# Reordering a latency-bound attention phase: a two-engine start, an earlier memory read, and segment boundaries without a drain

## Chip, cores and metric

The kernel runs on one core of one Trainium2 chip. The metric is the device time of one execution in microseconds (us), median over the runs of a kernel. Engines are named as in the profile: PE is TensorE (PEld its weight loads), DVE is VectorE, ACT is ScalarE, POOL is GpSimd, SP is the engine that issues the transfers. The granted clock is the share of PE's full clock that the profile shows as granted, averaged over a stretch.

## The reference

Two attention blocks read the same input and a gate mixes them:

```python
x = A_x                                             # [1, 2048, 512], bf16
g = sigmoid((x * gate_w).sum(-1, keepdims=True))
a = A_ref(...)   # memory transformer: 64 segments of 32 tokens + 8 memory tokens, 32 heads of 128, strictly serial
b = B_ref(...)   # infini-attention: 4 segments of 512 tokens, 32 heads of 16
return g * a + (1 - g) * b

# B_ref, for each of the 4 segments (M, z start at 0; phi(t) = t+1 if t > 0 else exp(t)):
p     = softmax(q k^T * scale + causal_mask);  a_dot = p v
a_mem = (phi(q) M) / (phi(q) z + 1e-6)
o     = sigmoid(beta) * a_mem + (1 - sigmoid(beta)) * a_dot
M    += phi(k)^T v;   z += sum(phi(k))
# then b = concat(o) @ wo
```

## The kernel before

The program first does all of B, then a barrier, then all of A. The change touches B and its start. Every operation is appended to a per-engine list in *program order*; a tracker derives the semaphore waits from what each operation reads and writes. An engine executes its own list strictly in order.

B works on 4 segments of 8 groups (4 heads each). One group needs: `pK`, `pQ`, `pV`, `pKr` (projections; `pKr` makes phi(k) and `pQ` makes phi(q)), three logits batches `w0`, `w1`, `w2` (each fills banks 0 to 3 of PSUM, the memory that matmuls write to, then four exps on ACT), `p` (P times V, into bank 4), `nz` (phi(q) times M and z, into bank 5), `mz` (update of M and z), and `chain` (8 small DVE steps that normalise and add).

```python
def plan_projQ(g):
    par = g % 2                                      # two buffers, by parity of the group
    P.op("pe", f_proj, ..., writes=[rbank[7]])       # 4 matmuls 128x512
    P.op("dve", copy pb[7] -> QTg[par])
    if sb > 0:
        P.op("dve", qmin[par] = min(QTg[par], 0))
        P.op("act", qmin[par] = exp(qmin[par]))
        P.op("dve", phiQ[par] = max(QTg[par], 0) + qmin[par])
# [cut]
def plan_nz(g):                                      # only where sb > 0
    pq = phiQ_b[g % 2]
    P.op("pe", f_nz, reads=[Rs("MZ16"), Rs("phiQ%d" % par)], writes=[rbank[5]])   # 16 matmuls 128x32
# [cut]
plan_proj(0)
for g in range(NG + 1):                              # NG = 8
    # order of one iteration (projections run one group ahead, P.V one group behind):
    #   w0(g)  pKr(g+1)  pK(g+1)  w1(g)  pQ(g+1)  p0(g-1)  w2(g)  p1(g-1)  nz(g-1)  pV(g+1)  mz(g)  chain(g-1)
    ...
for half in range(2):                                # end of a segment: orow -> oT, banks 6 and 7
    P.op("pe", f_otr, ...)                           # 8 transposes
    P.op("dve", ...)                                 # 2 copies
P.op("dve", MZ16 = bf16(MZ32))                       # if another segment follows
```

At the start, all 16 copies that spread the weights wq and wk into a padded layout stand on ACT, and `memT0` (transposed initial memory) follows the gate in DVE's order:

```python
for nat, pad, ... in ((wqN_sb, wqB_sb, ...), (wkN_sb, wkB_sb, ...)):
    for c in range(C):
        for half in range(2):
            P.op("act", lambda a: a.activation(pad[...], nat[...], ACT.Copy), ...)
# [cut: x transposes, gate matmul, gate sigmoid, omg, omgB]
P.op("pe", f_m0tr, ..., writes=[rbank[6]]);  P.op("dve", copy pb16[6] -> memT0)
```

The softmax here doesn't subtract the row's maximum and nothing guards it: scores larger than these inputs give would overflow.

## Time and profile before

| | before |
|---|---|
| time | 1735.62 us median of 4 runs (1733.33 to 1736.89) |
| span of the profiled run | 1733.5 us, mean granted PE clock 0.937 |
| first logits batch of B | 29.27 us |
| A starts (its first weight transfer is issued) | 351.66 us |
| period of a group, segments 0 / 1 / 2 / 3 | 7.16 / 10.27 / 10.33 / 8.82 us |
| boundaries, first batch of group 7 to first batch of the next segment's group 2 | 34.91, 37.30, 37.42 us |

The period is the distance between the first logits batches (`w0`) of groups 2 and 7, divided by 5; these start times are in the timeline. The other rows can be read there too.

The next view is the windows table of the kernel before: busy microseconds of each engine in a stretch (number of instructions in brackets), then granted clock, DMA share and GB/s. The rows are the groups of segments 1 and 3, and A.

```profile
core 0: us, PE busy (x) PEld busy (x) DVE busy (x) ACT busy (x) POOL busy (x), PEclk, DMA share, GB/s
...
97.50:166.00 68.50, 47.68 (x1007) 30.09 (x1010) 42.48 (x117) 44.30 (x100) 18.12 (x28) 0.83 0.01 2
...
274.60:336.50 61.90, 45.95 (x777) 27.04 (x784) 31.65 (x77) 41.47 (x92) 18.11 (x28) 0.65 0.01 2
378.00:1733.00 1355.00, 1296.69 (x32428) 997.10 (x32488) 522.08 (x1167) 521.61 (x1008) 115.01 (x250) 0.98 0.02 5
```

In the last row PE is busy for 1297 of 1355 us: A is PE-bound, and the change does not touch it. In the two rows above it no engine is full; in segment 1, of 68.5 us, PE is busy 47.7, DVE 42.5 and ACT 44.3. Something other than throughput sets the pace there.

The timeline of one group of segment 1 (start, duration, engine and line, operation, and in brackets how long the engine sat idle and for whom) shows the loop:

```profile
126.26 0.26 DVE L654 RECIPROCAL rden<-pb 128x16 f32<-128x16 f32 x1
...
129.63 0.43 DVE L548 SCALAR_TENSOR_TENSOR phiKg<-pb,Kmin 128x256 bf16<-128x256 f32 x1 [0.48 <-ACT Kmin L546]
...
130.12 1.04 PE L495 MATMUL pb<-xT,wqB_sb 128*128 128x512 bf16 x4 [0.56 <-DVE phiKg L548]
...
131.19 0.69 DVE L499 CAST QTg<-pb 128x512 bf16<-128x512 f32 x1 [0.54 <-PE pb L495]
...
131.91 0.71 DVE L505 TENSOR_SCALAR qmin<-QTg 128x512 bf16<-128x512 bf16 x1
...
132.66 0.63 ACT L507 ACTIVATE qmin<-qmin 128x512 bf16<-128x512 bf16 x1 [0.88 <-DVE qmin L505]
...
133.32 0.69 DVE L509 SCALAR_TENSOR_TENSOR phiQ<-QTg,qmin 128x512 bf16<-128x512 bf16 x1 [0.69 <-ACT qmin L507]
...
134.07 0.56 PE L619 MATMUL pb<-MZ,phiQ 128*128 128x32 bf16 x16 [1.14 <-DVE phiQ L509]
...
134.49 0.63 PE L520 MATMUL pb<-wvB_sb,xT 128*128 128x64 bf16 x16
...
135.28 0.43 PE L572 MATMUL pb<-QTg,KTg 16*128 16x128 bf16 x16
```

Each step begins when the one above it ends: `chain` on DVE (first line, 2.5 us to the end of its eighth step), Kmin and its exp (left out), phiK (L548), projQ (L495), copy of QT (L499), min (L505), exp on ACT (L507), phiQ (L509), then `nz` on PE (L619), which had waited 1.14 us for phiQ, then the V projection (L520), `mz` (left out here) and the next group's first logits (L572). The following `chain` starts at 136.35, 10.1 us after this one. PE takes part twice, with projQ and again with `nz`, V projection and `mz`; the second time it waits for phiQ only because `nz` stands ahead of the other two in its order. The group view says how much PE sat idle ahead of `nz` in all:

```profile
L619 PE MATMUL pb<-MZ,phiQ 128*128 128x32 bf16 x384 | 13.9, 182 | 15.6 <-DVE phiQ L509 15.5
```

That is 15.6 us of idle time over 24 executions, 15.5 of it for phiQ.

At a boundary the pipeline drains. This is the timeline of the second boundary, from the last group of segment 1 to the first of segment 2:

```profile
166.04 0.43 PE L572 MATMUL pb<-QTg,KTg 16*128 16x128 bf16 x16
...
175.56 1.25 PE L604 MATMUL pb<-V32g,PT_g 128*128 128x32 bf16 x40 [1.95 <-DVE adot L663]
...
179.77 1.89 PE L745 MATMUL pb<-ident,orow 128*128 128x128 bf16 x16 [2.44 <-DVE orow L675]
180.84 1.61 DVE L749 COPY oT<-pb 128x512 bf16<-128x512 bf16 x4 [1.13 <-PE pb L745]
...
182.05 1.49 PE L481 MATMUL pb<-xT,wkB_sb 128*128 128x512 bf16 x3 [0.40 <-DVE oT L749]
...
186.25 0.43 PE L572 MATMUL pb<-QTg,KTg 16*128 16x128 bf16 x16
```

After group 7's first logits (166.04) come the last P.V matmuls (L604), the transposes of the output (L745), their copies (L749), and only then the next segment's projections (L481) and first logits at 186.25.

And the start:

```profile
12.27 5.26 ACT L385 ACTIVATE wqB_sb<-wqN_sb 128x512 bf16<-128x512 bf16 x8 [10.19 <-DMA wqN_sb<-in_B_wq_dram]
...
17.44 5.24 ACT L385 ACTIVATE wkB_sb<-wkN_sb 128x512 bf16<-128x512 bf16 x8
...
24.41 0.17 DVE L452 COPY memT<-pb 128x32 bf16<-128x32 bf16 x1
...
25.11 1.49 PE L481 MATMUL pb<-xT,wkB_sb 128*128 128x512 bf16 x3 [5.20 <-DVE memT L452]
```

The 16 copies on ACT run one after the other (12.27 to 22.68), the gate sigmoids queue behind them, the copy of `memT0` (L452) queues behind the gate on DVE, and the first projection needs the bank that it frees. (The chain of waits shows none of this: it is followed back only to the transfers of Wv and Wo, which are issued when B ends.)

### The profile page before, as it was taken

The page shows a single profiled execution, that of the slowest core. Times are in us where ns is not written, and L with a number is a line of the kernel's source. Part 1 is how long each engine was busy: PE and PEld are TensorE (multiplying, and loading weights), DVE is VectorE, ACT ScalarE, POOL GpSimd, SP SyncE. Part 2 cuts the span into 40 slices and gives each one's busy share as a digit, 9 for nine tenths or more (in the row PEclk, how much of TensorE's full clock was granted, in tenths as well). Part 3 has the DMA queues.
Part 4 walks back from the last instruction along what each step waited for, and adds up shares of the span by engine and source line. Part 5 has one row for each costly group of instructions (what it writes and reads, how often), then busy time and mean ns, then how long its engine had stood idle before and what let it go on. Part 6 is the DMA issues. An engine that isn't in the chain of part 4 may idle for free.

```text
span 1733.5 us, 80136 instructions
## 1 busy us (share of the span) xinstructions
PE 1546.9 (89%) x37477; PEld 1161.6 (67%) x37573; DVE 722.5 (42%) x1727; ACT 735.5 (42%) x1477; POOL 203.6 (12%) x396
## 2 busy tenths in 40 slices
PE   5766666779999999999999999999999999999999
PEld 3444443467777777777777777777777777777776
DVE  3556665533333333333333333333333333333333
ACT  5756465624343334343333333433333333333333
POOL 1322122201010000000000000000000000000000
PEclk8977776589999999999999999999999999999999
DMA  7000000050000000000000000000000000000000
GB/s 292 3 2 2 2 2 2 2 196 3 6 3 6 3 6 3 6 3 7 3 6 3 6 3 6 3 7 3 6 3 6 3 6 3 6 3 6 4 6 6
DMA packets 12916, 28.22 MB, mean 16 GB/s; under 512 B 800, under 2 KB 11048, under 8 KB 11048
## 3 DMA queue, kind: packets, MB, share of 16 engines
q1 hardware_dynamic: 12584, 23.09, 3.6%
q8 instruction: 294, 4.82, 1.2%
q14 instruction: 38, 0.31, 0.1%
HBM read 20.99 MB, written 2.10 MB: 13 GB/s over the span
## 4 chain that ended last, share of the span: by engine, by line
PE 74%; DVE 3%; issue 1%; SPq 1%; DMA 1%
PE pb L867 26%; PE pb L801 24%; PE pb L929 14%; PE pb L853 4%; PE pb L916 3%; PE pb L822 3%; DVE aT_st L935 1%; DVE fin L996 1%; DMA Wo_sb<-in_A_Wo_dram 1%; SPq L310 1%; DVE t_sb L992 1%; DVE hT L785 0%; PE pb L950 0%; DVE V_sb L873 0%; DVE PT_sb L857 0%
## 5 line engine op out<-in xcount | busy, mean ns | idle before, releaser
L867 PE MATMUL pb<-Wv_sb,hT 128*40 128x512 bf16 x2048 | 497.8, 381 | 3.6 <-DMA Wv_sb<-in_A_Wv_dram 3.3
L876 ACT ACTIVATE V_sb<-pb 40x512 bf16<-40x512 f32 x448 | 264.8, 591 | 362.1 <-PE pb L867 362.1
L867 PEld LDWEIGHTS pb<-Wv_sb,hT 128*40 128x40 bf16 x2048 | 178.9, 99 | 174.5 <-DMA Wv_sb<-in_A_Wv_dram 3.4
L807 ACT ACTIVATE KT_sb<-pb 128x480 bf16<-128x480 f32 (+1 forms) x192 | 101.1, 527 | 395.9 <-PE pb L801 395.9
L811 DVE CAST QT_sb<-pb 128x480 bf16<-128x480 f32 (+1 forms) x192 | 115.7, 603 | 352.8 <-PE pb L801 345.1
L929 PE MATMUL pb<-OT_sb,Wo_sb 128*128 128x40 bf16 x8192 | 236.3, 183 | 17.5 <-DVE fin L996 16.4
L929 PEld LDWEIGHTS pb<-OT_sb,Wo_sb 128*128 128x128 bf16 x8192 | 225.0, 98 | 27.2 <-ACT OT_sb L920 17.8
L801 PE MATMUL pb<-hT,Wk_sb 128*128 128x40 bf16 x8192 | 216.5, 180 | 24.6 <-DVE hT L785 23.2
L801 PEld LDWEIGHTS pb<-hT,Wk_sb 128*128 128x128 bf16 x8192 | 210.7, 96 | 28.6 <-DVE hT L785 27.0
L801 PE MATMUL pb<-hT,Wq_sb 128*128 128x40 bf16 x8192 | 217.7, 179 | 3.0 <-issue 2.4
L801 PEld LDWEIGHTS pb<-hT,Wq_sb 128*128 128x128 bf16 x8192 | 211.2, 96 | 4.2 <-issue 3.4
L830 POOL TENSOR_SCALAR_AFFINE_SELECT P_sb<-P_sb 32x384 bf16<-32x384 bf16 (+1 forms) x192 | 98.7, 527 | 939.2 <-ACT P_sb L827 939.2
L581 ACT ACTIVATE PT_g<-pb 128x512 bf16<-128x512 f32 (+1 forms) x384 | 170.4, 529 | 54.5 <-PE pb L572 52.5
L835 DVE TENSOR_REDUCE rsum<-P_sb 40x12 f32<-40x480 bf16 (+1 forms) x192 | 112.0, 583 | 149.0 <-POOL P_sb L830 149.0
L935 DVE CAST aT_st<-pb 128x128 bf16<-128x128 f32 x64 | 18.7, 292 | 265.2 <-PE pb L929 265.2
L920 ACT ACTIVATE OT_sb<-pb 128x480 bf16<-128x480 f32 (+1 forms) x192 | 87.1, 526 | 94.6 <-PE pb L916 94.6
L840 DVE TENSOR_TENSOR Pn_sb<-P_sb,rrec 40x480 bf16<-40x480 bf16 (+1 forms) x192 | 118.9, 619 | 6.6
L853 PEld LDWEIGHTS pb<-ident,Pn_sb 40*40 40x40 bf16 x2048 | 63.5, 93 | 81.0 <-DVE PT_sb L857 33.7
L587 POOL TENSOR_SCALAR_AFFINE_SELECT PT_g<-PT_g 128x512 bf16<-128x512 bf16 x128 | 82.5, 644 | 257.7 <-ACT PT_g L581 255.6
L822 PEld LDWEIGHTS pb<-KT_sb,QT_sb 128*40 128x40 bf16 x2048 | 71.3, 98 | 30.0 <-issue 0.5
L827 ACT ACTIVATE P_sb<-pb 40x480 bf16<-40x480 f32 (+1 forms) x192 | 91.0, 507 | 0.0
L857 DVE COPY PT_sb<-pb 40x480 bf16<-40x480 bf16 (+1 forms) x192 | 70.1, 365 | 32.5 <-PE pb L853 32.5
(84 smaller groups left out, 1087.4 us busy)
## 6 DMA issues: line engine op xcount, KB each, us to landing
Wk_sb<-in_A_Wk_dram SPq DMA_DIRECT2D x4, 1024.0 KB, 12.0
Wq_sb<-in_A_Wq_dram SPq DMA_DIRECT2D x4, 1024.0 KB, 20.2
Wv_sb<-in_A_Wv_dram SPq DMA_DIRECT2D x4, 1024.0 KB, 9.2
Wo_sb<-in_A_Wo_dram SPq DMA_DIRECT2D x4, 1024.0 KB, 13.8
x_sb<-in_A_x_dram SPq DMA_DIRECT2D x4, 512.0 KB, 5.6
out_dram<-fin SPq DMA_DIRECT2D x16, 128.0 KB, 1.7
wqN_sb<-in_B_wq_dram SPq DMA_DIRECT2D x1, 512.0 KB, 7.8
wkN_sb<-in_B_wk_dram SPq DMA_DIRECT2D x1, 512.0 KB, 8.8
```

Source lines behind the costliest of these rows:

```text
L581: P.op("act", (lambda j=j: (lambda a: a.activation(ptb[:, j, 128 * n0:128 * (n0 + len(wv))], pb[j][:, 0:128 * len(wv)], ACT.Exp, scale=SCA ...
L801: ins = pe.matmul(pb[bnk][:, (h - h0) * L:(h - h0 + 1) * L], wsb[:, c, h * E:(h + 1) * E], hTc[:, c, :], start=(c == 0), stop=(c == C - 1))
L807: P.op("act", (lambda bnk=bnk, dst=dst, h0=h0, h1=h1: (lambda a: a.activation(dst[:, h0 * L:h1 * L], pb[bnk][:, 0:(h1 - h0) * L], ACT.Copy ...
L811: P.op("dve", (lambda bnk=bnk, dst=dst, h0=h0, h1=h1: (lambda dv: dv.tensor_copy(dst[:, h0 * L:h1 * L], pb[bnk][:, 0:(h1 - h0) * L])))(), ...
L822: ins = pe.matmul(pb[b][0:L, (h - h0) * L:(h - h0 + 1) * L], QT_sb[:, h * L:(h + 1) * L], KT_sb[:, h * L:(h + 1) * L], start=True, stop=True)
L830: P.op("gp", (lambda h0=h0, h1=h1, nh=nh: (lambda g: g.affine_select(P_sb[0:SEG, h0:h1, 0:SEG], P_sb[0:SEG, h0:h1, 0:SEG], [[0, nh], [-1, ...
L835: P.op("dve", (lambda h0=h0, h1=h1: (lambda dv: dv.tensor_reduce(rsum[0:L, h0:h1], P_sb[0:L, h0:h1, :], AX.X, ALU.add)))(), reads=[rP], wr ...
L840: P.op("dve", (lambda h0=h0, h1=h1, nh=nh: (lambda dv: dv.tensor_tensor(Pn_sb[0:L, h0:h1, :], P_sb[0:L, h0:h1, :], rrec[0:L, h0:h1].unsque ...
L853: ins = pe.transpose(dst, Pn_sb[0:L, h, :], ident[0:L, 0:L])
L867: ins = pe.matmul(pb[vb][0:L, 0:512], hTc[:, c, :], Wv_sb[:, c, 512 * j:512 * (j + 1)], start=(c == 0), stop=(c == C - 1))
L876: P.op("act", (lambda vb=vb, j=j: (lambda a: a.activation(V_sb[0:L, 512 * j:512 * (j + 1)], pb[vb][0:L, 0:512], ACT.Copy)))(), reads=[rban ...
L929: ins = pe.matmul(pb[6][:, c * L:(c + 1) * L], Wo_sb[:, h, c * 128:(c + 1) * 128], OT_sb[:, h * L:(h + 1) * L], start=(h == 0), stop=(h == ...
```

## The change

Its intent: use two engines for the weight copies and take `memT0` out of the gate's queue; read phi(q) before it is overwritten and not wait for a new one; and let the next segment's first projections, and the old segment's tail, run inside the normal groups.

```diff
-        for nat, pad, ... : (16 copies) P.op("act", ... activation(Copy))          # [cut]
+    # after the x transposes: wq copies on ACT and wk copies on POOL, alternating
+            for eng, nat, pad, rn, rp in (("act", wqN_sb, wqB_sb, ...), ("gp", wkN_sb, wkB_sb, ...)):
+                ...  activation(dst, srcn, ACT.Copy)   or   tensor_copy(dst, srcn)
+    # f_m0tr and memT0 moved ahead of the gate                                    # [cut]
@@ plan_bseg
-    def plan_projK(g): ... T0 ...          # and projQ, projV, projKr
+    def make_proj(psb):  T0p = psb * LB;  ...  return plan_projK, plan_projQ, plan_projV, plan_projKr
@@ order of an iteration
-    plan_proj(0)
-    for g in range(NG + 1):
+    if not v.get("B_proj_prefetched"): plan_proj(0)
+    nxt = make_proj(sb + 1) if sb + 1 < NB else None
+    old = v.get("B_tail")                  # the previous segment's p, nz, chain, transposes, MZ16 copy
+    for g in range(NG + (1 if nxt is None else 0)):
+        # in group 7 the projections are those of the next segment's group 0;
+        # in group 0 the p, nz and chain are those of the previous segment's group 7
             seq.append(("w", 1))
+        if g == 1 and old: seq.append(("otr", None))      # transposes, now in banks 4 and 5
+        if havep:          seq.append(("nz", None))       # moved: ahead of pQ
         if haven:          seq.append(("pQ", None))
 ...
             seq.append(("p", qc_parts[1]))
-            seq.append(("nz", None))
+            if g == 0: seq.append(("mz16", None))
-    (transposes and MZ16 copy at the end of each segment)
+    (transposes at the end of the last segment only)
```

A side effect: in the kernel before, `nz(g-1)` stands after `pQ(g+1)` in program order, and both use phiQ buffer `(g-1) % 2`. So for groups 0 to 5 it reads phi(q) of the wrong group. Every phi(q) is close to 1 with these inputs (by the scales in the reference, q has a standard deviation of about 0.0025), and the result still passes the comparison. The changed order reads the right one.

## The prediction

> **What bounds it now.** Two phases follow each other, with a barrier between. Infini-attention (B) runs to about 352 us, the recurrent memory transformer (A) to 1733. In the windows table PE is busy 95% from 378 us on at clock 0.98 to 0.99; the change leaves A alone. From the barrier to 377 us A waits for Wv and Wo, whose transfers are issued only after B (the chain of waits starts there), so whatever B saves moves everything after it by as much.
>
> In B no engine is full: PE 60 to 70%, DVE 48 to 61%, ACT 54 to 67% by quarter. It is latency-bound. From the timeline, first logits batch to first logits batch:
> - segment 0: 7.16 us a group, paced by ACT exps sharing four banks;
> - segments 1 and 2: 10.3 us, a loop: MZ update, DVE chain 2.5, Kmin, exp, phiK 1.25, projQ 1.05 (1.9 at half clock), QTg copy, min, exp, phiQ 2.8, then the nz matmuls (PE idles 32.9 us in total for phiQ), V projection, MZ matmuls, MZ update;
> - segment 3: mean 8.8 us.
> - Each boundary drains: group 7's first batch to the next segment's group 2 takes 34.9, 37.3 and 37.4 us.
> - Start: PE waits until 24.7 us; ACT makes 16 weight copies of 0.63 us, and the gate sigmoid, then memT0 on DVE, wait behind them.
>
> **What changes.**
> 1. Start: half the copies go to POOL, in parallel, and memT0 goes before the gate. wkN lands at 13.7 us; POOL takes 0.29 us for 128 columns, 0.64 for a 512-column select, so I estimate 0.7 to 1.0 per copy, ready by 19.5 to 22. The Trainium skill ("SBUF — State Buffer", Who interferes with whom) says DVE and GpSimd can block each other at a shared port; the DVE min at 0.29 us stretches to 0.76 next to a POOL select here. Gain 4.
> 2. nz moves before projQ. In program order the old nz(g-1) reads phiQ after group g+1 has overwritten it, so it waits for a value just made (and the wrong one; phi is near 1, which hides it). Now it reads one made an iteration earlier, in a gap where PE waited for phiK. The loop closes over DVE order instead: phiQ, V32g copy 0.42, MZ update 0.83: about 9.0 us. Five intervals each: 6.4 + 6.6 us in segments 1 and 2, about 3 in segment 3.
> 3. Boundaries: the next segment's group-0 projections ride in group 7, the old tail in the new group 0, the 16 transposes (1.9 us, with copies 1.6) in group 1, where they delay projQ by about 2.9; the MZ16 copy adds 0.7. Three iterations: about 27, 30.5 and 29. Gains 8, 6.7, 8.5.
> 4. Segment 3's end: nz(7) now stands before pv(7) and waits for the previous chain: loss 1.
>
> Sum 42 us, all on the critical path. Prediction **1693 us**, 80% range 1681 to 1706; faster by over 2% 0.76, within 2% 0.23, slower 0.01.
>
> **Right or wrong by:** A starting at about 310 us; first projection at about 21; segments 1 and 2 at about 9.0 us a group; waits for phiQ nearly gone; no 10 us ACT gap at boundaries; A unchanged.
>
> **What could spoil it.** POOL copies slower than 1.2 us; transposes stalling group 1 longer; clock: the Trainium skill ("TensorE: Matmul & The Clock Gate", Part 1) says the clock halves after an idle window and recovers with activity. The windows show 0.50 at the drains and 0.65 to 0.85 in the loops; shorter gaps may lift it (then 1683) or not (projQ costs 0.85 more in each group, then 1705).

One reading in it is too large: the 32.9 us is PE's wait and PEld's wait added up. PE's own is 15.5 us. No term of the sum used it.

## The result, and the profile after

| | before | after |
|---|---|---|
| time, median (range, runs) | 1735.67 us (1731.9 to 1739.29, 12) | 1689.56 us (1686.21 to 1695.64, 8) |
| ratio to before | 1 | 0.9736 (95% interval 0.9723 to 0.975) |
| span of the profiled run | 1733.5 us | 1689.7 us |
| first logits batch | 29.27 us | 24.73 us |
| A starts | 351.66 us | 306.00 us |
| period, segments 0 / 1 / 2 / 3 | 7.16 / 10.27 / 10.33 / 8.82 us | 7.37 / 9.03 / 9.09 / 8.26 us |
| boundaries | 34.91, 37.30, 37.42 us | 26.12, 30.67, 25.17 us |

A ratio is the mean time of one kernel's fast runs over that of the other's fast runs of the same rounds, so it is not quite the ratio of the medians.

The windows table after, same columns, for the corresponding stretches (segments 1 and 3, and A):

```profile
83.20:147.20 64.00, 48.94 (x1060) 32.98 (x1071) 45.79 (x130) 43.21 (x99) 18.36 (x29) 0.81 0.01 3
...
230.60:289.80 59.20, 42.47 (x854) 26.97 (x865) 38.97 (x102) 40.99 (x91) 18.06 (x29) 0.80 0.01 2
334.00:1689.00 1355.00, 1295.51 (x32391) 995.47 (x32451) 522.12 (x1167) 521.67 (x1008) 114.99 (x250) 0.99 0.02 5
```

A (last row) took nearly the same: 1296 us of PE busy in 1355. Its length from start to end was 1383.7 us, against 1381.8 before. All of the gain lies in B, after which A starts 45.66 us earlier. ACT's idle stretch at the three boundaries, 10.2 to 12.6 us before, was 2.7 to 3.9 us.

The same part of a group in segment 1, after:

```profile
120.41 0.26 DVE L665 RECIPROCAL rden<-pb 128x16 f32<-128x16 f32 x1
...
123.52 0.56 PE L630 MATMUL pb<-MZ,phiQ 128*128 128x32 bf16 x16
...
123.77 0.42 DVE L555 SCALAR_TENSOR_TENSOR phiKg<-pb,Kmin 128x256 bf16<-128x256 f32 x1 [0.48 <-ACT Kmin L553]
...
124.26 1.04 PE L502 MATMUL pb<-xT,wqB_sb 128*128 128x512 bf16 x4 [0.17 <-DVE phiKg L555]
...
127.37 0.69 DVE L516 SCALAR_TENSOR_TENSOR phiQ<-QTg,qmin 128x512 bf16<-128x512 bf16 x1 [0.69 <-ACT qmin L514]
...
127.98 0.42 DVE L531 CAST V32g<-pb 128x256 bf16<-128x256 f32 x1
128.32 0.83 DVE L653 TENSOR_TENSOR MZ<-MZ,pb 16x32 f32<-16x32 f32 x4
...
128.49 0.44 PE L583 MATMUL pb<-QTg,KTg 16*128 16x128 bf16 x16 [0.80 <-ACT PT_g L592]
```

`nz` (L630) now sits in front of projQ, in time that PE otherwise spent waiting for phiK (L555), and waits for nothing. The loop closes on DVE: phiQ (L516), V copy (L531), MZ update (L653), then the next `chain` at about 129.2. The group view of `nz`:

```profile
L630 PE MATMUL pb<-MZ,phiQ 128*128 128x32 bf16 x384 | 14.0, 182 | 5.7 <-DVE oT L715 3.4 <-DVE amem L683 2.3
```

None of its idle time is for phiQ any more; 3.4 us is for the copies of the transposes and 2.3 us for the end of the last segment. The start:

```profile
12.04 5.26 ACT L424 ACTIVATE wqB_sb<-wqN_sb 128x512 bf16<-128x512 bf16 x8 [9.96 <-DMA wqN_sb<-in_B_wq_dram]
...
13.59 5.35 POOL L426 COPY wkB_sb<-wkN_sb 128x512 bf16<-128x512 bf16 x8 [8.98 <-DMA wkN_sb<-in_B_wk_dram]
...
17.70 0.16 DVE L435 COPY memT<-pb 128x32 bf16<-128x32 bf16 x1
...
20.09 1.49 PE L488 MATMUL pb<-xT,wkB_sb 128*128 128x512 bf16 x3 [0.24 <-issue]
```

POOL's eight copies (13.59 to 18.94) run beside ACT's eight, `memT0` is done at 17.86, and projK's row starts at 20.09 instead of 25.11 (it shows three of the four matmuls: in both runs the record of the first is missing, and the weight loads for it start at 19.69 and 24.70). And the transposes in group 1 of segment 1:

```profile
95.23 1.40 PE L711 MATMUL pb<-ident,orow 128*128 128x128 bf16 x16
...
96.23 1.42 DVE L715 COPY oT<-pb 128x512 bf16<-128x512 bf16 x4 [0.77 <-PE pb L711]
...
97.70 0.56 PE L630 MATMUL pb<-MZ,phiQ 128*128 128x32 bf16 x16 [1.07 <-DVE oT L715]
...
98.33 0.81 PE L502 MATMUL pb<-xT,wqB_sb 128*128 128x512 bf16 x3
```

The transposes (L711) follow the second logits batch; `nz` then waits 1.07 us for their copies (L715), because it needs bank 5, and projQ (L502) stands behind `nz`.

### The profile page after: what moved, and what is told of

It is laid out like the page before. It is cut to its first block, busy times and chain, and to the rows that moved or that the text cites. A ratio compares the mean times of both kernels' runs of the same rounds, so it can differ in the third digit from the quotient of the medians.

```text
span 1689.7 us, 80119 instructions
## 1 busy us (share of the span) xinstructions
PE 1534.3 (91%) x37474; PEld 1157.7 (69%) x37573; DVE 726.0 (43%) x1727; ACT 730.1 (43%) x1469; POOL 208.9 (12%) x404
## 4 chain that ended last, share of the span: by engine, by line
PE 76%; DVE 3%; issue 1%; DMA 1%; SPq 0%
PE pb L905 28%; PE pb L839 25%; PE pb L967 14%; PE pb L891 4%; PE pb L954 3%; PE pb L860 3%; DVE aT_st L973 1%; DMA Wv_sb<-in_A_Wv_dram 1%; DVE fin L1034 1%; DVE t_sb L1030 1%; DVE hT L823 0%; PE pb L988 0%; DVE V_sb L911 0%; DVE PT_sb L895 0%; SPq L304 0%
```

## The experiments

The account to be tested: three parts act one after the other in time and their gains nearly add; inside a group the pace is a latency loop through DVE in program order, which the wait of `nz` for a new phiQ had lengthened. The main rival: what was gained is clock and fewer drains, and moving `nz` only moves a wait. (Periods and boundaries below are read from each run's timeline, as above.)

### 1. The start alone

```diff
  (kernel before)
- plan_init of before
+ plan_init of the changed kernel
```

> The kernel before with the first part of the change alone (half of the weight copies on POOL, the memory transpose ahead of the gate). My account, in which the parts act one after the other in time: the first logits batch at about 24.7 us instead of 29.3, everything after it moved by as much, total about 4.5 us less (1731). Rival, the gain of the whole change is one of clock and of fewer drains: the earlier start is eaten by a slower first segment (in the changed kernel segment 0 took 0.7 us more), total within 1 us of before.

Measured: 1731.87 us (6 runs, 1728.92 to 1736.11) against 1735.27 (11 runs), ratio 0.9979 (0.9958 to 1.0). The first logits batch came at 24.80 us, as expected. But the six times fall in two clusters, three near 1729 and three near 1735, and the profiled run was the slowest of them: it kept only 1.6 us up to the start of A. Its segment 1 took 72.23 us from group 0 to group 7 (68.45 before), and the granted clock over this stretch was 0.72 against 0.83. So the head start is real, and the profiled run lost most of it where its clock was low. Nothing shows that the new start causes this: the kernel before scatters as much (1729.67 to 1740.15), and the mean granted clock over all runs is 0.938 for both kernels. The medians differ by 3.4 us, but with an interval that reaches 1.0 this experiment does not settle what the start is worth.

### 2. nz moved, nothing else

```diff
  (kernel before)
+ nz(g-1) ahead of pQ(g+1)
- nz(g-1) after p1(g-1)
```

> The kernel before with the nz matmuls moved ahead of projQ, and nothing else. My account: the group period of segments 1 and 2 goes from 10.3 to about 9.0 us and that of segment 3 from 8.8 to about 8.3, which is 15 us over the three times five intervals, and each of the three drained segment ends loses about 1.2 us because nz of the last group now stands before its P.V matmuls and waits for the previous chain; net about 12 us less (1723 to 1724). Rival (clock and drains): the period stays above 10 us, since the drains that cool the clock are still there; total unchanged or 3 us more.

Measured: 1721.89 us (6 runs), ratio 0.9923 (0.9903 to 0.9944), so 13.4 us less. Periods 9.04, 9.11 and 8.30 in segments 1, 2 and 3: the changed kernel's own, to within 0.05, with all the drains still there. The clock over groups 2 to 7 of segments 1 and 2 was 0.81 and 0.83, against 0.77 and 0.74 before, so it has to be ruled out group by group: two groups of segment 1 at clocks of 0.76 and 0.77 took 8.98 us each here, while three at 0.83 took 10.10 to 10.13 us before. For these two segments the rival is out: the shorter period needs neither fewer drains nor more clock. For segment 3 it is not (see the table of terms below). The ends of segments 1, 2 and 3, from the first batch of group 7 on, became 0.9, 0.6 and 1.1 us longer, less than the 1.2 us each that was expected.

### 3. nz left late, but with three phiQ buffers

```diff
  (kernel before)
- phiQ_b = 2 buffers, index g % 2
+ phiQ_b = 3 buffers, index (sb * 8 + g) % 3, in pQ and in nz
```

> The kernel before with nz left in its old, late place, but with three phiQ buffers in place of two, so that it reads the value made one iteration earlier and never waits for the one just made. My account: it was the wait for the just-made phiQ and not the place in program order that lengthened the loop, so the period of segments 1 and 2 goes to 9.0 to 9.3 us and the drained ends lose nothing: about 13 to 15 us less (1721 to 1723), and the time in which PE waits for phiQ falls from 33 us to nearly 0. Rival: the place matters, because 0.56 us of matmuls now stand between the P.V matmuls and the next logits batch instead of in a gap; then the period is 9.6 or more and the gain under 8 us.

Measured: 1720.70 us (4 runs), ratio 0.9917 (0.9898 to 0.9937). Periods 9.43, 9.32 and 7.96. The group view of `nz` in this run:

```profile
L621 PE MATMUL pb<-MZ,phiQ 128*128 128x32 bf16 x384 | 13.9, 184 | 0.0
```

The wait is gone with the place unchanged, and the time that it cost is gone with it. It was the wait for a value just made, not the position. Position is worth second-order amounts in both directions: 0.2 to 0.4 us a group worse here in segments 1 and 2 (above my 9.3 for segment 1), 0.3 better in segment 3 (where the clock differed too, 0.79 against 0.71), and 1.3 us better at the end of the last segment (14.94 against 16.28 us).

### 4. The boundaries alone

```diff
  (changed kernel)
- plan_init of the changed kernel;  nz ahead of pQ
+ plan_init of before;              nz after p1, two phiQ buffers
```

> The changed kernel with the start of before and with nz in its old, late place: only the segment boundaries are pipelined. My account: the three boundaries, group 7 to group 2, go from 34.9, 37.3 and 37.4 us to about 27.5, 33.6 and 28.9, while the period inside segments 1 and 2 stays at 10.3 us: about 20 us less (1716). The three parts alone then sum to about 37 of the 46 us, and the rest is the interplay: with nz moved, the boundary groups shorten too and two of the three drained ends are gone. Rival (all of the gain is from drains and clock): 40 us or more from this part alone, with a period near 9.

Measured: 1710.17 us (4 runs), ratio 0.9855 (0.9836 to 0.9874), so 25 us less, more than the 20 expected. Boundaries 23.69, 31.27 and 28.12 us (I had 27.5, 33.6, 28.9); periods 10.72, 10.10 and 9.19, the slow ones. The boundary part and the period part are separate, as the account says. Boundary 0 is even shorter than the changed kernel's 26.12 us, because its group 1, with the transposes, took 8.9 us and not 11.2: the late `nz` does not stand between the transposes and projQ (experiment 6). The medians of the three parts alone give 3.4 + 13.4 + 25.1 = 41.9 us of the 46.1. With part 1 as uncertain as it is, no interplay has to be assumed beyond a few us.

### 5. The changed kernel with the old start

```diff
  (changed kernel)
- plan_init of the changed kernel
+ plan_init of before
```

> The changed kernel with the start of before put back (16 copies on ACT, memory transpose after the gate), everything else as changed. My account: the first logits batch again at about 29.3 us and the total about 4.5 us above the changed kernel (1694), so that the start is worth its 4.5 us there. In the first experiment the start alone moved the first batch by 4.5 us but the profiled run kept only 1.6 us of it, with the rest lost in segment 1 at a lower clock. Rival: that loss is the rule, and this kernel is within 1.5 us of the changed one.

Measured: 1695.43 us (5 runs, 1690.55 to 1699.79), ratio 0.9767 (0.9747 to 0.9787); the changed kernel's own ratio was 0.9736 and, in a later control, 0.9728. The start is worth 5 to 7 us here by these ratios, with intervals that still overlap a little (0.9723 to 0.975 and 0.9707 to 0.9748 for the changed kernel). First batch at 29.12 us. The profiled run nevertheless started A at 306.19 us, level with the changed kernel's, because in it four of the last five intervals in segment 3 took 7.4 us and not 8.5. The clock over these groups was 0.91, against 0.75 in the changed kernel: the scatter of the first experiment with the sign reversed.

### 6. The changed kernel with nz late and three phiQ buffers

```diff
  (changed kernel)
- nz ahead of pQ, two phiQ buffers
+ nz after p1, three phiQ buffers
```

> The changed kernel with nz in the old late place and three phiQ buffers. My account: like the changed kernel within 5 us (1685 to 1695), period of segments 1 and 2 at 9.0 to 9.4 us, PE waits for phiQ near 0: place is second order, the wait was what counted. Rival (place counts): 5 us or more slower than the changed kernel.

Measured: 1684.68 us (4 runs), ratio 0.9707 (0.9691 to 0.9724): about 5 us faster than the changed kernel, at the edge of what I had expected. Periods 9.20, 9.19, 7.64. The profile says where it came from. In group 1 of segment 1:

```profile
94.74 1.07 PE L713 MATMUL pb<-ident,orow 128*128 128x128 bf16 x16
...
95.40 1.42 DVE L717 COPY oT<-pb 128x512 bf16<-128x512 bf16 x4 [0.23 <-PE pb L713]
...
95.65 1.03 PE L502 MATMUL pb<-xT,wqB_sb 128*128 128x512 bf16 x4
...
98.05 0.55 PE L632 MATMUL pb<-MZ,phiQ 128*128 128x32 bf16 x16
```

projQ (L502) no longer has `nz` between itself and the transposes (L713), so it starts when they are issued and does not wait for their copies (L717); `nz` (L632) runs later. Group 1 took 9.33, 10.24 and 8.23 us in the three later segments, against 11.16, 12.74 and 10.40 in the changed kernel. The end took 14.93 us against 16.28. Segment 3's shorter period (7.64 against 8.26) is not put down to the order: its clock was 0.87 against 0.75, and experiment 5, with `nz` early, took 7.60 at 0.91.

### 7. PE kept busier

```diff
  (changed kernel, in nz)
+ 2 extra matmuls 128x512 into bank 5, which nz then overwrites
```

> The changed kernel with two extra 128x512 matmuls ahead of each nz batch in segments 1 to 3, whose results nz overwrites; they stand where PE waits for phiK, and keep it busier. It separates clock from latency. My account: the group is a latency loop in which the clock only touches projQ (1.04 or 1.9 us) and the short batches; the extra 0.43 us (0.85 at half clock) fits the gap of 0.6 to 1.3 us in full-clock groups but delays projQ in half-clock ones: total within 8 us of the changed kernel, either way. Rival (the clock is what made the change fast or keeps it from being faster): the granted clock between 100 and 290 us rises from about 0.82 to 0.95 or more and the total falls by 10 us or more.

Measured: 1695.34 us (4 runs), ratio 0.9767 (0.9753 to 0.9782): about 5 us slower. Two rows of the windows table for this run, groups 2 to 7 of segments 1 and 2 (columns as above; the clock is the third number from the end),

```profile
101.12:146.57 45.45, 34.39 (x771) 22.29 (x771) 33.96 (x95) 30.86 (x70) 13.01 (x20) 0.92 0.01 3
178.20:223.87 45.67, 34.56 (x771) 22.39 (x771) 34.30 (x95) 30.73 (x70) 13.02 (x20) 0.93 0.01 3
```

and for the changed kernel:

```profile
102.01:147.15 45.14, 34.59 (x756) 22.98 (x761) 33.54 (x95) 30.89 (x70) 13.21 (x20) 0.81 0.01 3
177.82:223.27 45.45, 34.65 (x756) 23.23 (x761) 34.07 (x96) 31.00 (x70) 13.30 (x20) 0.81 0.01 2
```

The clock rose from 0.81 to 0.92 and 0.93, short of the 0.95 that the rival named, yet the periods of segments 1 and 2 stayed at 9.09 and 9.13. Two groups of segment 1 that ran at full clock throughout took 9.02 us each, with projQ still waiting 0.85 us for phiK. Segment 3, where PE had less slack, went from 8.26 to 8.84 at nearly the same clock (0.77 and 0.75). In segments 1 and 2, more clock did not shorten the loop.

### 8. The chain split into DVE's waits

```diff
  (kernel of experiment 6)
- chain(g-1): 8 DVE steps in one piece at the end of iteration g
+ chain(g-2) in iteration g: 2 steps after Kmin, 1 after the KT copy, 2 after the min of Q, 3 after phiQ
- nz(g-1) after p1;  MZ16 single;  transposes in banks 4 and 5, after w1
+ nz(g-1) last;      MZ16 double;  transposes in banks 5 and 7, after pV
```

> The kernel of the run with late nz and three phiQ buffers, on top of the changed one, and in addition the 8 normalising DVE steps of a group are no longer done in one piece of 2.5 us ahead of Kmin: they are deferred by one group and put between the evictions, where DVE waits for ACT or PE (two after Kmin, one after the KTg copy, two after the min of Q, three after phiQ); MZ16 gets a second buffer. My account says that the loop runs through DVE in program order, with about 7.5 us of work and 1.5 us of waiting per group: filling the waits brings the period of segments 1 and 2 from 9.0 to about 8.0 to 8.4 us and the total to 1672 to 1682. Rival (ACT's exps over four shared banks, 7.2 to 7.6 us, or PE set the period): the period stays at 9 us and the total within 5 us of the changed kernel.

Measured: 1691.81 us (6 runs), ratio 0.9741 (0.9712 to 0.9771). The expected total failed. Periods of segments 1 and 2 were 8.63 and 8.33 us, one above the expected 8.0 to 8.4 and one within it, both below 9, so the loop does run through DVE's order (this run moved `nz` and the transposes as well, so the share of the split alone is not measured). The rival's total came true, within 5 us of the changed kernel, but not its period. One thing that worked against the split: the last step of the chain (`orow`) took 0.76 to 0.85 us in every group from 2 to 7 of these segments, where it began 0.06 to 0.15 us after a POOL select and ended 0.28 us after it; in the kernel before it took 0.42 to 0.44. But segment 3 rose to 8.29 (7.64 in experiment 6) and its boundary to 27.49 (24.46). The six times form two clusters: three at 1683 to 1687 with mean granted clocks of 0.958 to 0.963, and three at 1697 to 1698 with 0.949 to 0.952. I had left out that the last segment has no phiK loop to shorten, while `nz`, now last, waits there for the split chain (0.2 to 1.0 us in four of its groups). The granted clock from 235 to 290 us was also low, 0.72, so this run alone does not divide the loss between the two.

### 9 to 11. Control, repetition, and a mixed version, on one chip

```diff
  (9: changed kernel, unedited)   (10: kernel of experiment 6, unedited)
  (11: kernel of experiment 8)
- split chain and late transposes in all segments
+ split chain in segments 0 to 2;  chain in one piece, nz after p1, transposes after w1 in segment 3
```

> The changed kernel itself, unedited, as the control on the same chip as the next two. 1687 to 1693 us, ratio to before 0.972 to 0.976.

> The changed kernel with late nz and three phiQ buffers once more (it was 0.9707 of before, against 0.9736 of the changed kernel on another chip run). Its gain came, by the group times, from the boundaries' transpose group (9.3, 10.2 and 8.2 us in place of 11.2, 12.7 and 10.4: nz, which waits for the transposes' copies, no longer stands ahead of projQ) and from the end (14.9 in place of 16.3 us). If that holds it is 4 to 7 us faster than the control; if it was chance, within 2 us of it.

> The split-chain kernel, in which segments 1 and 2 fell to 8.3 to 8.6 us a group but segment 3 rose from 7.6 to 8.3 and its boundary from 24.5 to 27.5, with the split kept in segments 0 to 2 and the last segment as in the late-nz kernel. My account (the loop through DVE in program order binds where the phiK loop is there, and not in the last segment): segments 1 and 2 stay at 8.3 to 8.6, segment 3 returns to 7.6 and its boundary to about 25, total 5 to 9 us below the late-nz kernel (1676 to 1680). Rival (what the order gains is lost to the clock, which moves at random): no faster than the late-nz kernel.

| run | median (runs) | ratio to before (95%) | periods, segments 1 / 2 / 3 | boundaries | A starts |
|---|---|---|---|---|---|
| 9, changed kernel | 1688.34 (4) | 0.9728 (0.9707 to 0.9748) | 8.94 / 9.17 / 8.26 | 25.84, 30.33, 27.08 | 305.96 |
| 10, nz late, 3 buffers | 1683.10 (5) | 0.9695 (0.9672 to 0.9718) | 9.33 / 9.36 / 7.67 | 24.18, 28.62, 25.42 | 301.07 |
| 11, mixed | 1679.34 (4) | 0.9677 (0.9657 to 0.9698) | 8.60 / 8.40 / 7.86 | 25.71, 30.31, 26.35 | 297.54 |

The gain of experiment 6 repeated: 5.2 us below the control (the intervals still overlap a little). So did its sources: group 1 took 9.44, 10.24 and 9.96 us against the control's 11.08, 11.87 and 11.21, and the end 14.99 against 16.28. Run 11 is 9 us below the control with separate intervals; over run 10 it gained 3.8 us, less than the 5 to 9 expected, and those two intervals overlap. Its periods are the short ones of experiment 8, but its boundaries cost 0.9 to 1.7 us more than run 10's, and segment 3 and its boundary came to 7.86 and 26.35 us, not to the 7.6 and 25 expected.

## Why the prediction was right

The time (1689.56 us in a range of 1681 to 1706, forecast 1693) and the steps can be checked term by term, in the profiled runs. The terms measured are differences of first-batch times, so they add up exactly to the shift of A. They come from one profiled run of each kernel.

| term | predicted gain, us | measured, us |
|---|---|---|
| start | 4 | 4.54 |
| segment 0, groups 0 to 7 | 0 | -0.67 |
| boundary 0 | 8 | 8.79 |
| segment 1, five intervals | 6.4 | 6.23 |
| boundary 1 | 6.7 | 6.63 |
| segment 2, five intervals | 6.6 | 6.19 |
| boundary 2 | 8.5 | 12.25 |
| segment 3, five intervals | 3 | 2.83 |
| end of segment 3 | -1 | -1.13 |
| sum | 42 | 45.66 |

The match in segment 3 is partly luck. These are groups 2 to 7 of segment 3 in the kernel before and in experiment 1, which runs the same order there:

```profile
292.40:336.51 44.11, 33.91 (x598) 20.80 (x601) 25.17 (x65) 29.25 (x65) 12.99 (x21) 0.63 0.01 2
...
293.17:334.95 41.78, 30.63 (x598) 19.25 (x601) 24.97 (x65) 29.20 (x65) 13.08 (x21) 0.76 0.01 2
```

With a clock of 0.76 in place of 0.63, the old order took 2.33 us less. The changed kernel took 41.28 us at 0.75, and in experiment 5 the same order took 38.01 us at 0.91. So most of the 2.83 us may be clock, and what the move of `nz` is worth in this segment is not shown.

- **"The loop closes over DVE order instead ... about 9.0 us."** Right: 9.03 and 9.09, and again 9.04 and 9.11 with that one move alone (experiment 2). Experiment 3 shows the wait as its cause; experiments 8 and 11 show DVE's order as what remains. One cost in it was not foreseen: in six of the ten intervals counted, the chain's last step (`orow`) began 0.08 to 0.13 us after a POOL select, ended 0.28 us after it, and so took 0.78 to 0.83 us; these intervals took 9.02 to 9.63 us. In the other four it began before the select and took 0.42 us; they took 8.62 to 8.92. No run tests this by itself.
- **Start.** Right in mechanism and size at the first batch. The POOL copies took 0.61 us each, less than my 0.7 to 1.0. In the total of a single run it can be hidden by the clock (experiments 1 and 5).
- **"they delay projQ by about 2.9".** Right in the sum of boundaries 0 and 1. Group 1 took 11.16 and 12.74 us, so 2.1 and 3.7 above the 9.03 and 9.09 period. Experiment 6 showed what I had not said: most of that delay is not the transposes but `nz`, which waits for their copies ahead of projQ.
- **Boundary 2, "about ... 29"**: this is the term that was mis-sized. It measured 25.17 us (25.37 in experiment 5, 27.08 in run 9). If group 1 is given the 10.40 us that it took, 29 us leaves 9.3 us each for groups 7 and 0, as in a segment with the DVE loop; but the groups that prepare the last segment make no phiK. Group 7 there:

```profile
226.34 0.56 PE L630 MATMUL pb<-MZ,phiQ 128*128 128x32 bf16 x16
...
226.76 1.02 PE L502 MATMUL pb<-xT,wqB_sb 128*128 128x512 bf16 x4
...
230.65 0.44 PE L583 MATMUL pb<-QTg,KTg 16*128 16x128 bf16 x16 [0.17 <-ACT PT_g L592]
```

  projQ (L502) follows `nz` (L630) without a wait, and the group takes 7.38 us from its first logits at 223.27 to the next at 230.65, like a group of segment 0. So boundary 2 was 7.38 + 7.39 + 10.40. A part of the surplus may be clock: that was 0.93 over this boundary, and in run 9, at 0.75, group 7 took 8.48 us and the boundary 27.08, which is half-way back to 29.
- **End.** Right: `nz` ahead of the last P.V matmuls costs 1.13 us; it is back to 14.9 to 15.0 us where `nz` is late (experiments 3, 6, 10).
- **The clock.** The Trainium skill ("TensorE: Matmul & The Clock Gate", Part 1) says that K, the granted share, is either half or full and that a free-running window decides. The traces agree: the clock records of the kernels before and after hold 1.0 and 0.5 alone, in stretches that are whole multiples of 3.41 us but for the last. My "shorter gaps may lift it" came true in part. From the first logits batch to the start of A the mean clock went from 0.75 to 0.82: in segment 1's groups it was 0.83 before and 0.81 after, but in segment 3's it went from 0.65 to 0.80 and over boundary 2 from 0.64 to 0.93. So a part of the gain in segment 3 and boundary 2 may be clock, and whether the change or chance lifted it there is not shown. The clock remains the largest scatter between runs of one kernel seen here (up to 15 us in experiment 8), and which groups fall at half clock in a given run stays open.

## What to carry to other kernels

Where no engine is full, follow one loop through the timeline and ask of each step whether it has to wait for *this* value: a read placed behind the overwrite of its own buffer waits for the wrong producer, and moving it or adding a buffer removes the wait (both did here, 13 to 15 us). A drained boundary is worth the time that the next stage's first work could have overlapped; cost it by the period of the groups that do the work, and check that they have the same loop. A single run's few-us difference in such a phase may be clock, so ask of each event time whether it moves with the clock: the period of segments 1 and 2 was 8.94 to 9.17 us in all four profiled runs with the same order in them (changed kernel, experiments 2, 5 and 9), that of segment 3 was 7.60 to 8.30.

## What the Trainium skill lacked or had wrong

- "TensorE: Matmul & The Clock Gate" (Why this matters for your kernels) advises against PE gaps above about 3 us. In the changed kernel PE's longest idle time between 106 and 119 us was 0.80 us, and the granted clock still fell from 1.00 to 0.50 at about 116.5 us. The page's section "A second HAM failure mode" describes such oscillation; neither gives a busy share that avoids it, and the runs here only show that 0.75 (PE busy 52.7 of the 70 us from 100 to 170) did not.
- "GPSIMD Engine Reference" (3.1) gives about 1.8 cycles per element as the best case of a loop, 768 ns for 512 elements, while 4.1 calls one-input work "roughly line-rate". It has no figure for a bf16 `tensor_copy`: the strided copy of 512 elements per partition took 614 ns on POOL here, less than that best case and about as ACT's 629 ns.
- "SBUF — State Buffer" (Who interferes with whom): nothing wrong here. The page says that DVE and GpSimd can share a port pair and that whichever comes second is blocked until the other's instruction ends. The DVE min of 128x512, 0.29 us, took 0.71 us beside a POOL select in the group of the kernel before shown above, and up to 0.76 us elsewhere; in that run all nine stretched ones started after the select and ended 0.14 to 0.15 us after it.
